# A chain of attention, SwiGLU layer and gated product on one core: w1's second-half left factors made in the late stage, preparation steps held behind the main pipeline

## The chip, the cores and the metric

The kernel runs on one core of a Trainium2 chip. The metric is the device time of one execution in microseconds; before the change the median of 3 runs is 1453.51 us (1453.17 to 1454.55). Beside these runs one execution was recorded by the hardware profiler; the rows below come from it. The core's engines, each with a queue of its own that it works off in order: TensorE (PE, matmuls), VectorE (DVE), ScalarE (ACT), GpSimd (POOL) and SyncE (SP, which here only issues DMA transfers). ACT issues some transfers too.

## The reference

```python
a1 = softmax(p k^T / 8) v            # 32 packed rows per head; 8 batches, 8 heads, 576 rows, head_dim 64
x  = softmax(q a1^T / 8) a1          # then reshaped to 4608 x 512
h  = x @ w_in                        # 512 x 2048
x2 = (h * sigmoid(h)) @ w_out        # 2048 x 512
a, b = x2 @ w1, x2 @ w2              # 512 x 1024 each
out  = ((a * b) @ w3) @ w_out2       # 1024 x 1024, then 1024 x 512
```

All in float32. The kernel folds the last two weights into one, w34 = w3 @ w_out2, before it uses them.

## The kernel before

Every float32 matmul is done as three: each operand is split into a high part, which the engine takes at full pace, and the low part that is left (`split`: the high part a copy on ACT or, with `on_vector`, a cast on DVE; the low part a subtraction on DVE, or on POOL with `eng=G`), and `mm3` (L97) adds high x high, low x high and high x low.

**First product (attention and SwiGLU), to about 877 us.** The main loop runs over 256 items (b, f, m): batch, half of its 576 rows, and one of 16 blocks of 128 columns of w_in. For item i, `emit_h` makes h in a PSUM bank ps_h (6 matmuls of 288 columns), `emit_g` makes sg = tanh(h/2) on ACT, gg = (sg + 1) h on DVE (the gate), its high part gh on ACT and its low part gl on POOL, and `emit_x2` for item i - 3 adds gh and gl times w_out to four PSUM banks ps_x (12 matmuls). ps_h has two banks, so PE can be about two items ahead of the gate. `fetch` loads the left operands of h (mr) and splits them into the slots mq.

Beside the items run three streams of other work, called a step at a time by the loop at the pace of `due`. One is attention for later batches. In the z stream, `decode_late` turns the first MID = 20 blocks of a list `late` of weight blocks from packed 64-bit words to float32 and stores them to DRAM (late_d). From item 209 to item 250 the x stream runs `prepare_second` (L942), the **late stage**. Its `step` takes the next block of the list: it loads it (z from late_d, or raw words from the input, which `Decode` turns with two ACT copies, two DVE operations at L176 and L178, and a POOL add), and then

- a block of w_out2 ("o") is split into o, high part on DVE (tile wo in the rows),
- a block of w3 ("3") is kept for `turn`, which splits it into w3T, and `product`, which multiplies it with o on PE into ps_w: 12 matmuls of 512 columns per w3 block, 16 blocks; every second one is split into w34s and stored,
- a block of w1 or w2 ("12") is kept for `combine`, which with its partner makes the **left factors**: the second product multiplies 2 x 2 blocks with seven multiplications in place of eight (Strassen), for which each pair of blocks needs four sums (DVE, tile sums, L933) and seven parts. Each part is split (tile w12s: high part on ACT, low part on DVE) and stored to DRAM (w12_d) by a transfer that ACT issues. `later` holds these small steps, `some(2)` runs two of them at a time.

w1 and w2 have two column halves. Each half has four combines (w1 and w2, two row pairs each). The late stage makes those of the first half. The blocks of the second half are only decoded.

**Second product, from about 877 us.** 36 items (9 groups of 512 rows, 4 column pairs mp). `emit_ab` makes seven products (12 matmuls of 256 columns each) into ps_ab, sums them on DVE (r), multiplies a and b and splits the result (abh on ACT, abl on DVE); `emit_o` multiplies the previous item's with w34 into ps_o (24 matmuls of 512 columns). Column pairs 0 and 1 use the left factors of the first half, which `load_second` (L1126) loads. Those of pairs 2 and 3 (tile w_23) are made in place by `last_left_factors` (L1139) during the first two items, with the low parts on POOL, from decoded blocks that `load_z12` loads. The memory of w_23 comes free when the last xs of the first product has been stored.

**What sets the order.** A scheduler orders the instructions of each engine's queue by its own model of their times, within the data dependences. `tc.issue_after(ins)` adds that an instruction on the engine of `ins` stands behind `ins`. `behind` holds the latest of some of them: `behind["sg"]` the tanh, `behind["gg"]` the gate. The late stage's steps have no such bound before the change.

## Time and profile before

| what | value |
|---|---|
| median of 3 runs | 1453.51 us |
| profiled execution | 1451.29 us, of which the span from first to last instruction is 1449.5 us |
| PE busy | 1397.1 us (96%) |
| DVE busy | 908.6 us (63%) |
| ACT busy | 672.1 us (46%) |
| POOL busy | 598.6 us (41%) |
| mean granted TensorE clock | 0.991 of full |
| DMA | 193.07 MB, mean 133 GB/s |

Busy times are shares of the span; matmuls are pipelined and their recorded durations overlap, so PE counts as busy while it only works off what it holds, and its real pace is read from start to start. The granted clock of a stretch is a mean of the two levels of TensorE's clock, 2.4 GHz (1.00) and 1.2 GHz (0.50).

### The profile page before, as it was taken

What the parts mean: (1) busy time and instruction counts of PE and PEld (TensorE: products, weight loads), DVE (VectorE), ACT (ScalarE), POOL (GpSimd) and SP (SyncE); (2) the same over time, 40 slices, a digit from 0 to 9 for tenths busy, and PEclk for the clock granted to TensorE, in tenths of its full rate; (3) what the DMA queues carried; (4) which work ended last, traced back from release to release, by engine and by line L of the source; (5) the groups of instructions that cost most, each with busy time, mean ns of one, the idle gap of its engine ahead of it and who ended that gap; (6) DMA issues with size and microseconds to landing.
All of it is one profiled execution on the core that took longest, in us unless ns stands there. A gap on an engine that the chain in (4) does not pass through costs nothing.

```text
span 1449.5 us, 25884 instructions
## 1 busy us (share of the span) xinstructions
PE 1397.1 (96%) x9548; PEld 1310.8 (90%) x9548; DVE 908.6 (63%) x1695; ACT 672.1 (46%) x1466; POOL 598.6 (41%) x626
## 2 busy tenths in 40 slices
PE   7799899999999999999989999999999999999998
PEld 5488799899999999999878998899999999999998
DVE  5897866569775588667897435745364454545453
ACT  6866555565665556654465433422132232323221
POOL 3778755856879657686476333300000000000000
PEclk9999999999999999999999999999999999999999
DMA  8597545845567444562686339011010101101000
GB/s 317 192 311 247 170 140 168 264 139 151 161 205 226 142 134 141 168 181 86 231 267 203 108 133 355 9 59 30 30 59 1 59 12 48 48 12 59 1 30 30
DMA packets 135967, 193.07 MB, mean 133 GB/s; under 512 B 14496, under 2 KB 92576, under 8 KB 135328
## 3 DMA queue, kind: packets, MB, share of 16 engines
q1 hardware_dynamic: 125344, 178.82, 38.4%
q10 hardware_dynamic: 10496, 12.59, 2.5%
q8 instruction: 75, 1.23, 0.3%
q14 instruction: 52, 0.43, 0.1%
HBM read 132.38 MB, written 58.98 MB: 132 GB/s over the span
## 4 chain that ended last, share of the span: by engine, by line
PE 68%; DVE 12%; DMA 7%; ACT 5%; issue 4%; POOL 2%; SPq 2%; ACTq 0%; DVEq 0%; POOLq 0%
PE ps_ab L1225 24%; PE ps_x L100 5%; PE ps_x L98 5%; PE ps_x L99 5%; PE ps_o L98 5%; PE ps_o L99 5%; PE ps_o L100 5%; PE ps_h L98 3%; PE ps_h L100 3%; PE ps_h L99 3%; DVE gg L838 1%; SPq L108 1%; DMA z<-late_d 1%; DVE sbd L244 1%; DVE mq L86 1%
## 5 line engine op out<-in xcount | busy, mean ns | idle before, releaser
L98 PE MATMUL ps_x<-gh,wo 128*128 128x288 f32 x1024 | 303.2, 300 | 6.2 <-DVE xs L875 2.0
L99 PE MATMUL ps_x<-gh,wo 128*128 128x288 f32 x1024 | 301.3, 297 | 0.0
L100 PE MATMUL ps_x<-gl,wo 128*128 128x288 f32 x1024 | 285.9, 298 | 2.3 <-POOL gl L91 2.2
L91 POOL TENSOR_TENSOR gl<-gg,gh 128x288 fp32r<-128x288 f32 x256 | 227.5, 892 | 110.9 <-ACT gh L82 94.9
L1225 PE MATMUL ps_ab<-xct,w 128*128 128x256 f32 x1728 | 222.3, 283 | 1.4 <-DVE r L1246 1.4
L1225 PEld LDWEIGHTS ps_ab<-xct,w 128*128 128x128 f32 x1728 | 214.9, 190 | 2.6 <-DVE r L1246 1.6
L98 PEld LDWEIGHTS ps_x<-gh,wo 128*128 128x128 f32 x1024 | 194.3, 190 | 11.4 <-DVE xs L875 3.6
L82 ACT ACTIVATE gh<-gg 128x288 fp32r<-128x288 f32 x256 | 112.7, 443 | 183.1 <-DVE gg L838 174.5
L99 PEld LDWEIGHTS ps_x<-gh,wo 128*128 128x128 f32 x1024 | 194.4, 190 | 2.2 <-issue 1.2
L100 PEld LDWEIGHTS ps_x<-gl,wo 128*128 128x128 f32 x1024 | 187.7, 190 | 5.5 <-POOL gl L91 4.3
L91 POOL TENSOR_TENSOR mq<-mr,mq 128x256 fp32r<-128x256 f32 x168 | 131.2, 781 | 113.7 <-DVE mq L86 47.1
L1225 PE MATMUL ps_ab<-xcb,w 128*128 128x256 f32 x1296 | 177.2, 283 | 0.0
L98 PE MATMUL ps_h<-a,mq 128*128 128x288 f32 x512 | 156.5, 306 | 21.4 <-DVE gg L838 17.2
L838 DVE SCALAR_TENSOR_TENSOR gg<-sg,ps_h 128x288 f32<-128x288 f32 x256 | 114.5, 447 | 96.1 <-ACT sg L833 48.8
L1225 PEld LDWEIGHTS ps_ab<-xcb,w 128*128 128x128 f32 x1296 | 168.1, 189 | 4.3
L1246 DVE TENSOR_TENSOR r<-p,ps_ab 128x512 f32<-128x512 f32 x72 | 49.2, 683 | 182.9 <-PE ps_ab L1225 182.7
L99 PE MATMUL ps_h<-a,mq 128*128 128x288 f32 x512 | 152.4, 298 | 0.0
L100 PE MATMUL ps_h<-a,mq 128*128 128x288 f32 x512 | 152.0, 297 | 0.1
L833 ACT ACTIVATE sg<-ps_h 128x288 f32<-128x288 f32 x256 | 102.7, 404 | 62.1 <-PE ps_h L100 44.1
L98 PEld LDWEIGHTS ps_h<-a,mq 128*128 128x128 f32 x512 | 96.8, 189 | 30.9 <-DVE gg L838 24.0
L82 ACT ACTIVATE p<-ps_ab 128x512 f32<-128x512 f32 x72 | 43.1, 598 | 145.5 <-PE ps_ab L1225 139.1
L99 PE MATMUL ps_o<-w,abl 128*128 128x512 f32 x280 | 110.0, 393 | 0.0
(173 smaller groups left out, 2649.2 us busy)
## 6 DMA issues: line engine op xcount, KB each, us to landing
mr<-m_d SPq DMA_DIRECT2D x144, 128.0 KB, 2.6
raw<-in_moe_w_dram SPq DMA_DIRECT2D x32, 512.0 KB, 4.4
wz<-wi_d SPq DMA_DIRECT2D x48, 256.0 KB, 3.7
m_d<-ms SPq DMA_DIRECT2D x96, 128.0 KB, 3.0
x_d<-xs SPq DMA_DIRECT2D x20, 576.0 KB, 3.6
raw<-in_moe_w_out_dram SPq DMA_DIRECT2D x22, 512.0 KB, 4.2
out_dram<-ob SPq DMA_DIRECT2D x36, 256.0 KB, 2.0
vr<-in_v_dram SPq DMA_DIRECT2D x14, 640.0 KB, 4.1
```

What stands on the lines that cost most here:

```text
L82: A.activation(out=dst, in_=src, func=ACTF.Copy, scale=mul)
L86: V.tensor_copy(out=hi, in_=src)
L91: (eng or V).tensor_tensor(out=lo, in0=src, in1=hi.bitcast(F32), op=ALU.subtract)
L98: T.matmul(out=dst, lhsT=wh, rhs=xh, start=start, stop=False)
L99: T.matmul(out=dst, lhsT=wl, rhs=xh, start=False, stop=False)
L100: T.matmul(out=dst, lhsT=wh, rhs=xl, start=False, stop=stop)
L108: return eng.dma_start(out=out, in_=in_)
L244: (act_copy if plain else V.tensor_copy)(dst[r, 0, :, r], src[r])
L833: ins = A.activation(out=sg, in_=ps, func=ACTF.Tanh, scale=0.5)
L838: ins = V.scalar_tensor_tensor(out=gg, in0=sg, scalar=1.0, in1=ps, op0=ALU.add, op1=ALU.mult)
L1225: T.matmul(out=bank[:, x], lhsT=w[:, wp], rhs=xt[:, kt, xp], start=first and (x, kt, n) == (0, 0, 0), stop=last and (x, kt, n) == (1, 1, 2 ...
L1246: V.tensor_tensor(out=dst, in0=p, in1=q, op=op)
```

## The change

The list `late` begins with only KEPT = 4 blocks that wait for the second product, those of w2's second half. The four w1 blocks of the second half join the ones that the late stage combines: 6 combines there in place of 4, 2 in the second product in place of 4. w12_d becomes one tensor per half, and `load_second` also loads w1's part for column pairs 2 and 3. The high parts of o move from DVE to ACT. New: `hold(...)` puts a step's instructions behind the latest tanh and gate (and, for `turn` and `product`, behind the latest matmul into ps_h); `due_w3` takes a step only when the w3 block that is needed next is behind it in the list; `some(3)` in place of `some(2)`; and the last left factors run two steps per turn, not four.

```diff
@@ -97,9 +97,16 @@
     def mm3(dst, wh, wl, xh, xl, start, stop):
         T.matmul(out=dst, lhsT=wh, rhs=xh, start=start, stop=False)
         T.matmul(out=dst, lhsT=wl, rhs=xh, start=False, stop=False)
-        T.matmul(out=dst, lhsT=wh, rhs=xl, start=False, stop=stop)
+        return T.matmul(out=dst, lhsT=wh, rhs=xl, start=False, stop=stop)
 
     behind = {}
+
+    def hold(*names):
+
+        stack = ExitStack()
+        for x in names:
+            stack.enter_context(tc.issue_after(behind[x]))
+        return stack
 
     def move(out, in_, eng=DMA):
 
@@ -131,7 +138,7 @@
     ident = const.tile([128, 128], F32, name="ident")
 
     wi_d = dram.tile([4, DM, 512], F32, name="wi_d")
-    w12_d = dram.tile([128, 2, 2, 2, 7, 2, 128], F32, name="w12_d")
+    w12_d = [dram.tile([128, 2, 2, 2, 7, 2, 128], F32, name=f"w12_d{half}") for half in range(2)]
     w34_d = [dram.tile([128, 2, 512], F32, name=f"w34_d{i}") for i in range(KM2)]
     late_d = [dram.tile([128, 512], F32, name=f"late_d{n}") for n in range(MID)]
     x2_d = {(b, f): dram.tile([128, CD, HS], F32, name=f"x2_d{b}_{f}") for b in range(B) for f in range(2)}
@@ -821,11 +828,12 @@
         ps = ps_h.tile([128, HS], F32, tag="h", name="ps_h")
         w = slots[:, holds.index((b, m))]
         for x in range(2):
-            mm3(
+            ins = mm3(
                 ps, w[:, x, 0], w[:, x, 1],
                 a2[b][:, x, 0, f * HS:(f + 1) * HS], a2[b][:, x, 1, f * HS:(f + 1) * HS],
                 x == 0, x == 1,
             )
+        behind["h"] = ins.ins
         return ps
 
     def emit_g(i, ps):
@@ -886,16 +894,19 @@
         late_srcs.append((w1, w2)[x][128 * c:128 * c + 128, 512 * half:512 * half + 512])
 
 
-    for n in range(KM2, 2 * KM2):
+    KEPT = 4
+    for n in range(2 * KM2 - KEPT, 2 * KM2):
         late_w12(n)
     for j in range(KM2):
         late.append(("o", j))
         late_srcs.append(wo2[128 * j:128 * j + 128, :])
+    due_w3 = []
     for n in range(2 * KM2):
         late.append(("3", n))
         late_srcs.append(w3[n])
-        if n % 2 == 0:
-            late_w12(n // 2)
+        due_w3.append(len(late) - KEPT)
+        if n % 4 < 3:
+            late_w12(n // 4 * 3 + n % 4)
 
     def decode_late():
 
@@ -947,7 +958,7 @@
             ps_dec, ps_w = bank("ps_dec"), bank("ps_w34")
 
             def load():
-                n = len(zs) + KM2
+                n = len(zs) + KEPT
                 if n < MID:
                     zs.append(dp.tile([128, 512], F32, tag="z", name="z", bufs=6))
                     move(out=zs[-1], in_=late_d[n])
@@ -962,12 +973,12 @@
             def combine(n):
                 z = [z12.pop(2 * n + y) for y in range(2)]
                 sums = dp.tile([128, 4, 256], F32, tag="sums", name="sums", bufs=2)
-                x, kt = divmod(n, 2)
+                half, x, kt = n // 4, n // 2 % 2, n % 2
 
                 def part(j, src):
                     t = dp.tile([128, 2, 2, 128], F32R, tag="w12s", name="w12s", bufs=4)
                     split(t[:, :, 0], t[:, :, 1], src.rearrange("p (j n) -> p j n", j=2))
-                    store(out=w12_d[:, :, x, kt, j], in_=t, age=0)
+                    store(out=w12_d[half][:, :, x, kt, j], in_=t, age=0)
 
                 later.extend(left_factors(z, sums, part))
 
@@ -980,13 +991,13 @@
             def step():
                 n = used[0]
                 used[0] += 1
-                while len(zs) < min(n + 3, len(late) - KM2):
+                while len(zs) < min(n + 3, len(late) - KEPT):
                     load()
-                (kind, i), z = late[n + KM2], zs[n]
-                if n + KM2 >= MID:
+                (kind, i), z = late[n + KEPT], zs[n]
+                if n + KEPT >= MID:
                     z = Decode(z, dp.tile([128, 512], I32, tag="z", name="z", bufs=6), ps_dec).z
                 if kind == "o":
-                    split(o[i][:, 0], o[i][:, 1], z, on_vector=True)
+                    split(o[i][:, 0], o[i][:, 1], z)
                 elif kind == "3":
                     z3[i] = z
                 else:
@@ -1013,17 +1024,20 @@
                     move(out=w34_d[i], in_=t)
 
             for n in range(KM2 + 3):
-                step()
+                with hold("sg", "gg"):
+                    step()
                 yield
             for n in range(2 * KM2 + 2):
-                if n > 1:
-                    product(n - 2)
-                if n < 2 * KM2:
-                    turn(n)
+                with hold("sg", "gg", "h"):
+                    if n > 1:
+                        product(n - 2)
+                    if n < 2 * KM2:
+                        turn(n)
                 for y in range(2):
-                    if used[0] < min(len(late) - KM2, KM2 + 3 + 3 * (n + y) // 2):
-                        step()
-                    some(2)
+                    with hold("sg", "gg"):
+                        if used[0] < (due_w3[min(n + 1 + y, 2 * KM2 - 1)] if n < 2 * KM2 - 2 else len(late) - KEPT):
+                            step()
+                        some(3)
                     yield
             some(len(later))
             flush()
@@ -1124,8 +1138,9 @@
             w34[m] = pool.tile([128, 2, 512], F32R, name=f"w34_{m}")
 
     def load_second(mp):
-        for x in range(2) if mp < 2 else ():
-            move(out=w12[mp][:, x], in_=w12_d[:, mp, x])
+        half, j = divmod(mp, 2)
+        for x in range(2 - half):
+            move(out=w12[mp][:, x], in_=w12_d[half][:, j, x])
         for m in pair(mp):
             move(out=w34[m], in_=w34_d[m])
 
@@ -1138,8 +1153,8 @@
 
     def last_left_factors():
 
-        for n in range(4):
-            x, kt = divmod(n, 2)
+        for n in range(2):
+            x, kt = 1, n
             sums = early.tile([128, 4, 256], F32, tag="sums", name="sums")
 
             def part(j, src):
@@ -1149,8 +1164,6 @@
             for step in left_factors([z12h.pop((n, y)) for y in range(2)], sums, part):
                 step()
                 yield
-            if n < 2:
-                load_z12(n + 2)
 
     def pair(mp):
         half, j = divmod(mp, 2)
@@ -1234,7 +1247,7 @@
         g, mp = items2[i]
         nxt = iter(())
         if i < 2:
-            nxt = (None for _ in range(7) if drain(islice(last_left, 4)) is None)
+            nxt = (None for _ in range(7) if drain(islice(last_left, 2)) is None)
         if mp == MP - 1 and g + 1 < NG:
             nxt = right_factors(g + 1)
         b1, b2, b3, b4 = (ps_ab.tile([128, 2, 256], F32, tag=f"ab{j}", name=f"ps_ab{j}") for j in range(4))
```

How this moves instructions, at three places. `gg<-sg,ps_h` is the gate on DVE; wo are the tiles o, the numbers behind names are the program's.

DVE where the late stage begins, before the change:

```order
L838 SCALAR_TENSOR_TENSOR gg<-sg,ps_h 128x288
L86 CAST wo_0_9878<-z 128x512
L91 TENSOR_TENSOR wo_0_9878<-z,wo_0_9878 128x512
L838 SCALAR_TENSOR_TENSOR gg<-sg,ps_h 128x288
L86 CAST wo_1_9879<-z 128x512
L86 CAST wo_2_9880<-z 128x512
L91 TENSOR_TENSOR wo_1_9879<-z,wo_1_9879 128x512
L86 CAST wo_3_9881<-z 128x512
L91 TENSOR_TENSOR wo_2_9880<-z,wo_2_9880 128x512
L838 SCALAR_TENSOR_TENSOR gg<-sg,ps_h 128x288
```

and with it:

```order
L846 SCALAR_TENSOR_TENSOR gg<-sg,ps_h 128x288 x5
L86 CAST mq<-mr 128x2x128
L91 TENSOR_TENSOR wo_0_9879<-z,wo_0_9879 128x512
L91 TENSOR_TENSOR wo_1_9880<-z,wo_1_9880 128x512
L846 SCALAR_TENSOR_TENSOR gg<-sg,ps_h 128x288
L86 CAST mq<-mr 128x2x128
L883 TENSOR_SCALAR xs<-ps_x_9396 128x288
L91 TENSOR_TENSOR wo_2_9881<-z,wo_2_9881 128x512
```

The casts are gone from DVE, the first low part stands four gates later, and then about one stands between two gates.

DVE with the change, the densest pass of the late stage, between the gates of items 229 and 230:

```order
L846 SCALAR_TENSOR_TENSOR gg<-sg,ps_h 128x288
L944 TENSOR_TENSOR sums<-z 128x256
L86 CAST mq<-mr 128x2x128
L91 TENSOR_TENSOR w3T<-z,w3T 128x512
L183 TENSOR_SCALAR z<-ps_dec 128x512
L185 SCALAR_TENSOR_TENSOR raw<-ps_dec,raw 128x512
L944 TENSOR_TENSOR sums<-z 128x256
L91 TENSOR_TENSOR w12s<-z,w12s 128x2x128 x2
L944 TENSOR_TENSOR sums<-sums,z 128x256
L183 TENSOR_SCALAR z<-ps_dec 128x512
L185 SCALAR_TENSOR_TENSOR raw<-ps_dec,raw 128x512
L944 TENSOR_TENSOR sums<-z,sums 128x256
```

Two more w12s low parts follow before the next gate, fourteen operations in all. The longest such list before the change has fourteen too, between the gates of items 218 and 219.

ACT where the second product begins, before the change:

```order
L82 ACTIVATE w_23_12001<-z_11767 128x2x128
L82 ACTIVATE w_23_12001<-z_11769 128x2x128 x2
L82 ACTIVATE w_23_12001<-sums 128x2x128 x4
L82 ACTIVATE w_23_12001<-z_11771 128x2x128
L82 ACTIVATE w_23_12001<-z_11773 128x2x128 x2
L82 ACTIVATE abh<-r_12019 128x512
L82 ACTIVATE abh<-r_12018 128x512
L82 ACTIVATE r_12189<-ps_ab_12185 128x2x256
L82 ACTIVATE w_23_12001<-sums 128x2x128 x4
```

and with it:

```order
L82 ACTIVATE w_23_12076<-z_11842 128x2x128
L82 ACTIVATE w_23_12076<-z_11844 128x2x128 x2
L82 ACTIVATE w_23_12076<-sums 128x2x128 x4
L82 ACTIVATE w_23_12076<-z_11846 128x2x128
L82 ACTIVATE abh<-r_12096 128x512
L82 ACTIVATE abh<-r_12095 128x512
L82 ACTIVATE w_23_12076<-z_11848 128x2x128 x2
L82 ACTIVATE r_12234<-ps_ab_12230 128x2x256
L82 ACTIVATE w_23_12076<-sums 128x2x128 x4
```

Eight high parts of left factors stand before abh, not ten, and behind these rows there are none left, where before the change fourteen more followed the first fourteen.

## Rows read from the trace of the kernel before

**Rows 1.** Windows: us; busy (count) of PE, PEld, DVE, ACT, POOL; clock; DMA share; GB/s.
```profile
690.00:782.00 92.00, 82.66 (x507) 75.52 (x507) 85.28 (x141) 52.70 (x119) 57.14 (x57) 0.94 0.77 254
782.00:860.00 78.00, 78.00 (x503) 73.04 (x503) 32.95 (x68) 31.52 (x71) 33.89 (x41) 1.00 0.29 97
690.00:860.00 170.00, 160.66 (x1008) 148.55 (x1008) 118.23 (x208) 84.22 (x189) 91.03 (x97) 0.97 0.55 182
876.00:892.00 16.00, 16.00 (x135) 16.00 (x134) 7.02 (x13) 3.60 (x7) 0.05 (x1) 1.00 1.03 393
892.00:916.00 24.00, 20.64 (x115) 18.31 (x114) 16.86 (x21) 11.64 (x31) 21.30 (x24) 0.86 0.49 180
```

**Rows 2.** Timeline of PE around 848 us: start, duration, instruction.
```profile
845.12 0.39 PE L98 MATMUL ps_w<-wo,w3T 128*128 128x512 f32 x1
...
847.85 0.30 PE L98 MATMUL ps_h<-a,mq 128*128 128x288 f32 x1
...
850.23 0.29 PE L98 MATMUL ps_h<-a,mq 128*128 128x288 f32 x1
```

**Rows 3.** Timeline of DVE, gates of items 205 and 250.
```profile
690.08 0.46 DVE L838 SCALAR_TENSOR_TENSOR gg<-sg,ps_h 128x288 f32<-128x288 f32 x1 [0.78 <-ACT sg L833]
...
859.31 0.45 DVE L838 SCALAR_TENSOR_TENSOR gg<-sg,ps_h 128x288 f32<-128x288 f32 x1 [1.93 <-ACT sg L833]
```

**Rows 4.** Groups of DVE, shapes apart, from 690 to 860 us: busy us, mean ns.
```profile
L838 DVE SCALAR_TENSOR_TENSOR gg<-sg,ps_h 128x288 f32<-128x288 f32 x46 | 20.5, 446 | 18.0 <-ACT sg L833 11.5 <-issue 4.5 <-POOL gl L91 2.0
L86 DVE CAST mq<-mr 128x256 fp32r<-128x256 f32 x32 | 17.6, 551 | 2.8 <-DMA mr<-m_d 2.8
L91 DVE TENSOR_TENSOR w12s<-sums,w12s 128x256 fp32r<-128x256 f32 x16 | 14.1, 907 | 0.0
L91 DVE TENSOR_TENSOR w3T<-z,w3T 128x512 fp32r<-128x512 f32 x16 | 14.1, 885 | 8.0 <-ACT w3T L82 8.0
L176 DVE TENSOR_SCALAR z<-ps_dec 128x512 int32<-128x512 int32 x20 | 13.6, 680 | 0.3 <-ACT ps_dec L82 0.2
L178 DVE SCALAR_TENSOR_TENSOR raw<-ps_dec,raw 128x512 int32<-128x512 int32 x20 | 13.5, 677 | 0.0
L91 DVE TENSOR_TENSOR w12s<-z,w12s 128x256 fp32r<-128x256 f32 x12 | 7.2, 616 | 0.8 <-ACT w12s L82 0.8
L91 DVE TENSOR_TENSOR wo<-z,wo 128x512 fp32r<-128x512 f32 x8 | 6.6, 823 | 0.1
L933 DVE TENSOR_TENSOR sums<-z 128x256 f32<-128x256 f32 x8 | 6.5, 821 | 3.0 <-POOL z L182 3.0
L86 DVE CAST wo<-z 128x512 fp32r<-128x512 f32 x8 | 4.3, 543 | 3.2 <-DMA z<-late_d 3.2
L933 DVE TENSOR_TENSOR sums<-sums,z 128x256 f32<-128x256 f32 x4 | 2.8, 695 | 0.0
L933 DVE TENSOR_TENSOR sums<-z,sums 128x256 f32<-128x256 f32 x4 | 2.2, 540 | 0.0
```

**Rows 5.** Tile w12s: duration in ns, minimum, median and maximum.
```profile
L108 ACTq DMA_DIRECT2D w_d<-w12s x28: 520/521/893, 711.8 to 812.4; - x28
L82 ACT ACTIVATE w12s<-sums x16: 400/418/421, 710.0 to 809.8; 128x256 fp32r<-128x256 f32 x16
L91 DVE TENSOR_TENSOR w12s<-sums,w12s x16: 411/878/1535, 717.4 to 811.7; 128x256 fp32r<-128x256 f32 x16
```

**Rows 6.** Timeline of PE at the change of stages.
```profile
897.72 2.04 PE L98 MATMUL ps_o<-w,abh 128*128 128x512 f32 x4 [2.00 <-ACT abh L82]
...
910.34 3.73 PE L1225 MATMUL ps_ab<-xct,w 128*128 128x256 f32 x19 [1.36 <-DVE r L1246]
```

**Rows 7.** Timeline of ACT at the change of stages.
```profile
893.97 1.03 ACT L82 ACTIVATE w<-z 128x256 fp32r<-128x256 f32 x3 [1.88 <-DMA x_d<-xs]
...
897.05 1.14 ACT L82 ACTIVATE abh<-r 128x512 fp32r<-128x512 f32 x2
```

**Rows 8.** DMA issues: KB each, median us from issue to landing.
```profile
w<-w_d SPq DMA_DIRECT2D x4, 1792.0 KB, 13.9
```

## The prediction, made before the changed kernel had run

> **What bounds the kernel now.** I read the windows by stage first, then TensorE's timeline, then the groups of VectorE (DVE), then the waits at the change of stages. TensorE (PE) is the bound almost everywhere: from 782 to 860 us it is busy all the time at a granted clock of 1.00 [rows 1]. Two places are not like that. From 690 to 782 us DVE is busy 85.28 of 92 us while PE is idle 9.3 us and its granted clock is 0.94, a mean of 1.2 and 2.4 GHz [rows 1]. From 892 to 916 us, where the second product begins, PE is busy 20.64 of 24 us at 0.86 [rows 1].
>
> How much time do they lose? PE's own pace is read where it never waits: 12 matmuls of 512 columns take 847.85 - 845.12 = 2.73 us, 18 of 288 columns 850.23 - 847.85 = 2.38 us [rows 2]. One pass over an item (6 matmuls into ps_h, 12 into ps_x) is 2.38 us. Between the gate of item 205 at 690.08 and that of item 250 at 859.31 us [rows 3] (counted back from item 255, the last) lie 45 passes and all 16 w3 products: 45 x 2.38 + 16 x 2.73 = 150.8 us of PE work in 169.2 us. **Lost in the late stage: 18.4 us**, and before 782, as PE is full behind it.
>
> Why: the stretch's preparation stands on DVE's queue in front of the gates. In the old order the eight casts of w_out2, their low parts, decodes and left factors stand up to fourteen between two gates from item 205 on, long before the products need them. PE then waits for gg. Behind 782 us DVE is busy only 32.95 of 78 us [rows 1]: the work is there, but too early.
>
> At the change of stages PE waits 2.00 us for abh and 1.36 us for DVE's r [rows 6]. ACT had stood until 893.97 us for the store of xs, then ran ten copies into w_23 before abh at 897.05 [rows 7]. The second wait stems from the same left factors: DVE's sums, which wait for POOL's low parts, stand in front of r.
>
> **The change part by part.**
>
> *Holding the steps and due_w3.* Every preparation instruction now stands behind the latest tanh on ACT, gg on DVE and ps_h group on PE, and steps are taken when a w3 block needs them. In the new order DVE has five gates in a row where the casts began, and one low part of wo2 per pass afterwards. From item 205 to 219 DVE's list is 20.1 us long (14 gates, 10 mq, 8 wo2 low parts, 2 xs, 1 w3T, each by its row [rows 4], xs priced as a gate) against 14 x 2.38 = 33.3 us of PE: no loss there.
>
> *Eight wo2 casts go from DVE to ACT.* 8 x 0.543 = 4.3 us leave DVE [rows 4]. ACT, busy 84.22 of 170 us [rows 1], hides 8 copies of at most two 256-wide ones each, 0.84 us [rows 5]; without that cover they would cost 6.7 us.
>
> *Two more combines in the late stage.* DVE gets 14 low parts (8 x 0.907 + 6 x 0.616 = 11.0 us) and 8 sums (4 x 0.821 + 2 x 0.695 + 2 x 0.540 = 5.8 us) [rows 4]; ACT 14 high parts at 0.418 and 14 store issues at 0.521 us, 13.1 us together [rows 5]. Net on DVE +12.5 us: its list from item 205 to 250 grows from 131.3 us (rows 4, and 8 w34s and 6 xs priced as L178 and gg) to 143.8 us. As neighbours overlap, 131.3 of listed time were 118.23 us of busy time [rows 1], a factor of 0.90, so 129 us against 150.8 us of PE. It fits as a whole, but not everywhere. From item 219 to 247 the new order puts on DVE 28 gates, 20 mq, 24 and 18 low parts of w12s, 24 sums, 15 w3T, 20 + 20 decode steps, 7 w34s and 4 xs: 120.6 us listed, 108.5 us net. PE has 28 x 2.38 + 15 x 2.73 = 107.6 us there. So DVE and PE are level for 28 passes; in the densest pass fourteen operations stand between two gates. Waits come on top. In the old stretch DVE was idle 92 - 85.28 = 6.7 us, 7% [rows 1], and its excess over PE plus these waits made the loss. Scaled to 108.5 us these are 7.9 us: 0.9 + 7.9, **I take 8.8 us lost** in place of 18.4, as the old stretch is the nearest row there is. Gain 9.6. Ends: 1 us lost (the excess alone) and 18 (as before).
>
> The price of those DVE ops is where the doubt is. The low part of w12s takes 411 ns at least, 878 in the middle, 1535 at most [rows 5]. The Trainium skill (SBUF — State Buffer, Who interferes with whom) says that a VectorE instruction with two SBUF inputs and a GpSimd instruction that reads SBUF exclude each other, the later one standing fully blocked; it speaks against putting more such work beside a busy GpSimd. By that rule the added ops are to be priced with their stretched durations; the sum by it is the one made here, 1440.4 us, and without it that of the rival "bare" below, 1432.6 us. This trace agrees with it: 411 against 1535 ns for one shape.
>
> *SP and DMA in the late stage.* Four more loads of decoded blocks and 14 more stores of 256 KB, 4.7 MB in 170 us, beside 182 GB/s moved and a DMA share of 0.55 [rows 1]: hidden. POOL's work there is unchanged.
>
> *Late decoding.* The same 20 blocks are decoded early, in another order; nothing is added, 0 us.
>
> *The second product.* 14 copies on ACT, 14 low parts on POOL, 8 sums on DVE and 4 loads go. The new ACT order has eight copies into w_23 before abh, not ten: 0.6 us earlier at some 0.31 us from copy to copy (ten from 893.97 to 897.05 [rows 7]). The wait for the xs store ahead of them stays, so most of the first PE wait stays. The second wait goes: fewer sums stand before r, and POOL ends 14 parts sooner. PE loses there 3.4 us idle plus up to 3.4 us of work at 1.2 GHz (0.86 over 24 us is 6.7 us at half pace) [rows 1, 6]. Half of both, about 3, and 0.5 make **3.5 us gained**. Ends: 6.8, and a loss, from the new loads: two of 1792 KB for w1's part stand on SP behind the xs store. The first is third in line, 2816 KB, 7.3 us at 393 GB/s [rows 1], so at 901.3 us at the earliest. PE wants it after the 24 ps_o matmuls and 12 of 256 columns: 897.7 + 5.5 + 1.4 = 904.6. If it lands as slowly as such loads did, 13.9 us from issue [rows 8], it comes at 908 us: PE waits 3.5 us, and as much again goes at the lower clock behind it. The lower end is -3.5.
>
> Sum: 9.6 + 3.5 = 13.1 us. The profiled execution took 1451.29 us (span 1449.5 and 1.8 around it): 1438.2. The median of the runs is 2.2 us higher, 1453.51, so **1440.4 us**.
>
> **The rivals.**
>
> "Bare": the stretched durations ease, as gates and POOL's parts no longer pile up. With the 42 low parts and 24 sums at 0.41 in place of 50.1 us the list is 97.6, net 87.8 against 107.6: 1 us lost, gain 17.4 + 3.5, **1432.6**. For it: PE and DVE would drift apart only seldom. Against: POOL's parts in these passes stay the same in number.
>
> "Given back": waits between ACT and DVE double. Each of the 42 stores on ACT stands behind its low part on DVE, and tanh and gh stand behind the store; 0.9 + 15.8 = 16.7 us are lost in the late stage, and the 1792 KB load comes late enough to eat the 3.5 us: 18.4 - 16.7 = 1.7, **1451.8**. For it: ACT and DVE both have over 40 more instructions where PE has least slack. Against: in the old stretch ACT was busy 52.70 of 92 us [rows 1].
>
> "Blocked": slower. DVE and POOL take turns so often in items 219 to 247 that the 66 low parts and sums, 0.76 us on average [rows 4], take 1.15: 70.5 + 75.9 = 146.4 listed, 131.8 net, 24.2 over PE; with 7.9 us of waits 32.1 us are lost, 13.7 more than now, less 3.5: **1463.7**. It turns slower by over 0.2% where 18.4 + 3.5 + 2.9 = 24.8 us are lost, 124.5 net, 138.3 listed: at a mean of 1.03 us. For it: single ones reach 1.535 us [rows 5]. Against: a mean a third above the one measured, with no more POOL work than before.
>
> "Not done": the queues keep the hoisted order. Against it stands the order itself; if so, 1453.
>
> **How the numbers follow.** Forecast (1434 to 1447) 0.60, bare 0.20, given back 0.12, blocked 0.06, not done 0.02. Range 1431 to 1450: it takes in bare and most ways between the forecast and given back; left out are blocked, not done and most of given back, some 0.18. A measurement here can tell about 0.2%, 2.9 us. Faster: forecast, bare and a quarter of given back, 0.83; same 0.10; slower 0.07.
>
> **What would show it.** Right: from 690 to 720 us PE busy throughout; DVE near 100% from about 730 to 835 rather than 700 to 780; gates one by one, not in pairs; 42 w12s stores; the span between gates 205 and 250 near 159 us; at the second product one wait for abh of about 1.5 us and none for r. Wrong: the stretch of items 219 to 247 taking over 120 us, a granted clock under 0.95 there, w12s low parts over 1 us on average, or PE waiting for the 1792 KB loads.

## The result, and the profile after

The changed kernel took 1438.99 us (median of 4 runs, 1435.87 to 1440.92), the kernel before beside it 1453.34 us: a ratio of 0.990, 95% interval 0.988 to 0.992. The forecast was 1440.4 us, range 1431 to 1450. The profiled execution took 1435.87 us, with a span of 1434.1 us.

The windows of the kernel after, with the columns of [rows 1] (busy time and count of PE, PEld, DVE, ACT, POOL, then clock, DMA share, GB/s):
```profile
690.00:720.00 30.00, 30.00 (x228) 30.00 (x227) 14.53 (x31) 15.11 (x37) 19.98 (x22) 1.00 0.69 228
720.00:782.00 62.00, 60.08 (x379) 56.17 (x379) 53.97 (x98) 37.05 (x88) 40.04 (x39) 0.97 0.74 235
782.00:860.00 78.00, 75.34 (x477) 70.17 (x476) 58.08 (x104) 43.68 (x101) 39.64 (x40) 0.98 0.68 227
690.00:860.00 170.00, 165.41 (x1080) 156.35 (x1079) 126.58 (x232) 95.83 (x223) 99.66 (x101) 0.98 0.71 230
878.00:902.00 24.00, 22.20 (x156) 20.50 (x156) 15.41 (x21) 10.04 (x23) 11.87 (x14) 1.00 0.88 340
```
From 690 to 720 us PE is full; before the change it was busy 27.87 of these 30 us. DVE's work is spread: 53.97 of 62 us and then 58.08 of 78, in place of 85.28 of 92 and then 32.95 of 78 [rows 1]. The change of stages (last row) keeps the clock at 1.00, where it was 0.86.

The gates of items 205, 219, 247 and 250, DVE's timeline of the kernel after (start, duration, instruction, and in brackets idle time before it and what ended that):
```profile
689.12 0.46 DVE L846 SCALAR_TENSOR_TENSOR gg<-sg,ps_h 128x288 f32<-128x288 f32 x1 [0.78 <-ACT sg L841]
...
722.44 0.45 DVE L846 SCALAR_TENSOR_TENSOR gg<-sg,ps_h 128x288 f32<-128x288 f32 x1 [1.14 <-POOL mq L91]
...
838.93 0.45 DVE L846 SCALAR_TENSOR_TENSOR gg<-sg,ps_h 128x288 f32<-128x288 f32 x1 [3.34 <-ACT sg L841]
...
848.89 0.46 DVE L846 SCALAR_TENSOR_TENSOR gg<-sg,ps_h 128x288 f32<-128x288 f32 x1 [1.93 <-ACT sg L841]
```
From 205 to 250 it is 848.89 - 689.12 = 159.8 us, where it was 169.2 [rows 3]: 9.5 us less, and 9.0 us over PE's own 150.8. All of that is lost behind item 219: from 205 to 219 PE's pace is kept (33.3 us for 14 passes of 2.38), from 219 to 247 it is 116.5 us against 107.6. From gate 250 to the end it is 1434.1 - 848.89 = 585.2 us, before 1449.5 - 859.31 = 590.2: 5.0 us less. The two gains make 14.5 us, as the medians do (14.4); the profiled executions lie 15.4 us apart, of which 1.0 stands before gate 205.

DVE's groups for the left factors of the kernel after, from 690 to 860 us (busy us, mean ns, idle before), which answer to [rows 4]:
```profile
L91 DVE TENSOR_TENSOR w12s<-sums,w12s 128x256 fp32r<-128x256 f32 x24 | 15.8, 678 | 1.3 <-ACT w12s L82 1.3
L91 DVE TENSOR_TENSOR w12s<-z,w12s 128x256 fp32r<-128x256 f32 x18 | 13.2, 749 | 0.0
L944 DVE TENSOR_TENSOR sums<-z 128x256 f32<-128x256 f32 x12 | 7.7, 642 | 0.6 <-POOL z L189 0.6
L944 DVE TENSOR_TENSOR sums<-sums,z 128x256 f32<-128x256 f32 x6 | 4.7, 783 | 0.0
L944 DVE TENSOR_TENSOR sums<-z,sums 128x256 f32<-128x256 f32 x6 | 2.5, 414 | 0.0
```
Counts times means, as in the prediction, these 66 operations are 44.6 us, 0.68 each. And the waits of PE at the change of stages, which answer to [rows 6]:
```profile
886.96 1.20 PE L98 MATMUL ps_o<-w,abh 128*128 128x512 f32 x4 [1.54 <-ACT abh L82]
...
897.40 3.14 PE L1238 MATMUL ps_ab<-xct,w 128*128 128x256 f32 x24 [0.26 <-DVE r L1259]
```

### The profile page after: what moved, and what is told of

Same layout as the page of the kernel before. It is cut to its first block, busy times and chain, and to the rows that moved or that the text cites. A ratio compares the mean times of both kernels' runs of the same rounds, so it can differ in the third digit from the quotient of the medians.

```text
span 1434.1 us, 25927 instructions
## 1 busy us (share of the span) xinstructions
PE 1390.1 (97%) x9548; PEld 1307.3 (91%) x9548; DVE 903.1 (63%) x1701; ACT 672.7 (47%) x1474; POOL 592.0 (41%) x612
## 4 chain that ended last, share of the span: by engine, by line
PE 68%; DVE 12%; DMA 6%; ACT 5%; issue 5%; POOL 2%; SPq 2%; ACTq 0%; DVEq 0%; POOLq 0%
PE ps_ab L1238 24%; PE ps_x L100 6%; PE ps_x L98 5%; PE ps_x L99 5%; PE ps_o L98 5%; PE ps_o L99 5%; PE ps_o L100 5%; PE ps_h L98 3%; PE ps_h L100 3%; PE ps_h L99 3%; SPq L115 2%; DMA m_d<-ms 1%; DVE gg L846 1%; DVE sbd L251 1%; DMA z<-late_d 1%
## 5 line engine op out<-in xcount | busy, mean ns | idle before, releaser
L100 PE MATMUL ps_x<-gl,wo 128*128 128x288 f32 x1024 | 289.5, 297 | 1.5 <-POOL gl L91 1.4
L1238 PE MATMUL ps_ab<-xct,w 128*128 128x256 f32 x1728 | 219.4, 282 | 0.3 <-DVE r L1259 0.3
L82 ACT ACTIVATE gh<-gg 128x288 fp32r<-128x288 f32 x256 | 112.7, 443 | 167.2 <-DVE gg L846 157.3
L91 POOL TENSOR_TENSOR mq<-mr,mq 128x256 fp32r<-128x256 f32 x168 | 136.7, 814 | 115.4 <-DVE mq L86 57.5
L100 PE MATMUL ps_o<-w,abh 128*128 128x512 f32 x280 | 109.5, 391 | 0.0
```

The source lines that it names most:

```text
L82: A.activation(out=dst, in_=src, func=ACTF.Copy, scale=mul)
L91: (eng or V).tensor_tensor(out=lo, in0=src, in1=hi.bitcast(F32), op=ALU.subtract)
L100: return T.matmul(out=dst, lhsT=wh, rhs=xl, start=False, stop=stop)
L1238: T.matmul(out=bank[:, x], lhsT=w[:, wp], rhs=xt[:, kt, xp], start=first and (x, kt, n) == (0, 0, 0), stop=last and (x, kt, n) == (1, 1, 2 ...
```

## The experiments

All are told by the same two stretches of their profiles, gate 205 to gate 250 (PE's own work in it is 150.8 us in each) and gate 250 to the end, since where gate 205 lies differs by up to 4 us between executions (689.1 to 692.8 in those of kernels that differ only behind it). Ratios are to the kernel before, run beside them.

Two columns say where the first stretch loses: "PE idle", the waits of PE that the profile lists in it, and "clock", the stretch times what its mean granted clock is short of 1.00. What is left beyond 150.8 us and these two, 0.8 to 4.1 us, no row tells. They are those of the one profiled execution; the mean clock of whole executions differs within a kernel (e7: 0.990 to 0.994). How well do the stretches repeat? f1 and f3 differ only behind gate 250 and take 154.5 and 154.9 us to it; the eight kernels with the second product of the change take 584.8 to 586.7 us behind it.

| kernel | 205 to 250 | PE idle | clock | 250 to end | median | ratio, 95% interval |
|---|---|---|---|---|---|---|
| before | 169.2 | 9.2 | 5.1 | 590.2 | 1453.34 | |
| after | 159.8 | 4.6 | 3.4 | 585.2 | 1438.99 | 0.9901 (0.9879 to 0.9924) |
| e1_no_hold | 168.3 | 11.0 | 3.4 | 585.2 | 1448.21 | 0.9968 (0.9956 to 0.9981) |
| e2_hold_only | 153.8 | 2.0 | 0.0 | 590.2 | 1439.10 | 0.9907 (0.9893 to 0.9920) |
| e3_kept8 | 153.8 | 1.9 | 0.0 | 591.0 | 1438.81 | 0.9904 (0.9890 to 0.9917) |
| e4_cast_dve | 159.7 | 4.6 | 3.4 | 586.5 | 1437.24 | 0.9891 (0.9878 to 0.9905) |
| v3_spread | 157.2 | 3.6 | 0.0 | 584.8 | 1434.17 | 0.9871 (0.9857 to 0.9886) |
| e8_some2 | 158.5 | 4.0 | 1.7 | 585.2 | 1437.20 | 0.9891 (0.9873 to 0.9909) |
| e5_half_pool | 157.3 | 4.5 | 0.0 | 586.7 | 1438.00 | 0.9902 (0.9885 to 0.9918) |
| e7_store_sp | 154.7 | 2.6 | 0.0 | 585.4 | 1434.95 | 0.9877 (0.9862 to 0.9892) |
| f1_spread_sp | 154.5 | 2.4 | 0.0 | 585.2 | 1432.99 | 0.9868 (0.9850 to 0.9886) |
| f2_kept8_sp | 151.8 | 0.2 | 0.0 | 590.8 | 1437.53 | 0.9899 (0.9881 to 0.9917) |
| f3_later | 154.9 | 2.8 | 0.0 | 586.8 | 1433.76 | 0.9869 (0.9853 to 0.9885) |

### Which part of the change pays

**e1_no_hold**, the change without its hold:
```diff
     def hold(*names):
-        stack = ExitStack()
...
-        return stack
+        return ExitStack()
```


> The changed kernel with hold() doing nothing; all else stays (late factors, due steps, casts on ACT). Theory (the order on DVE makes the late gain): DVE's list from item 205 to 230 is 90.7 us again, 81.6 net, against 73.2 us of PE work, and with waits 17 to 22 us are lost from gate 205 to 250 (span 168 to 173 us); the second product keeps its 5 us: 1447 to 1453 us. Rival (less work on DVE, the casts and the pace, makes the gain, not the order): 1439 us as the changed kernel, span 159.8 us.

Measured: 168.3 and 585.2 us, 1448.21 us. DVE's gates of items 205 and 219 in its timeline:
```profile
692.58 0.45 DVE L843 SCALAR_TENSOR_TENSOR gg<-sg,ps_h 128x288 f32<-128x288 f32 x1 [0.78 <-ACT sg L838]
...
743.03 0.44 DVE L843 SCALAR_TENSOR_TENSOR gg<-sg,ps_h 128x288 f32<-128x288 f32 x1
```
They lie 50.5 us apart, not 33.3, and the second did not wait for an input: DVE itself was late. PE takes 45.0 us from its item 205 to its item 219, since it can run two items ahead of the gate. Without the hold 17.5 us are lost in the late stage, within the theory's 17 to 22, and 0.9 us of its gain are left; the 5 us of the second product stay.

**e2_hold_only**, the kernel before with nothing but the hold lines of the diff:
```diff
...
-                step()
+                with hold("sg", "gg"):
+                    step()
...
+                with hold("sg", "gg", "h"):
...
+                    with hold("sg", "gg"):
...
+                        some(2)
```


> The kernel before with hold() alone: the old steps, casts on DVE, four blocks of left factors of w1 and w2 still in the second product. Theory (order): list of items 219 to 247 is 102.2 us, 92 net against 107.6 us of PE, so only waits are lost: 3 to 8 us from gate 205 to 250 (span 154 to 159 us); the second product takes 590 us from gate 250 as before: 1439 to 1443 us. Rival (less work makes the gain): span 166 us or more, 1450 us or more.

**e3_kept8**, the change with w1's second half left in the second product:
```diff
-    KEPT = 4
+    KEPT = 8
...
-        if n % 4 < 3:
-            late_w12(n // 4 * 3 + n % 4)
+        if n % 2 == 0:
+            late_w12(n // 2)
...
-                        some(3)
+                        some(2)
...
-        for x in range(2 - half):
+        for x in range(2 if half == 0 else 0):
...
-        for n in range(2):
-            x, kt = 1, n
+        for n in range(4):
+            x, kt = divmod(n, 2)
...
+            if n < 2:
+                load_z12(n + 2)
...
-            nxt = (None for _ in range(7) if drain(islice(last_left, 2)) is None)
+            nxt = (None for _ in range(7) if drain(islice(last_left, 4)) is None)
```


> The changed kernel with w1's second half left in the second product (KEPT = 8, load_second and last_left_factors as before): hold, due steps and casts on ACT stay. Theory (the moved factors cost a little late and pay at the second product): span of gates 205 to 250 154 to 158 us, 2 to 5 us less than the changed kernel; from gate 250 to the end 590 us, 5 more; 1438 to 1442 us. Rival (the moved factors cost nothing late): span 159.8 us, 1444 us. Second rival (the second product gained by something else than the moved factors, such as the clock): 585 us from gate 250, 1434 to 1437 us.

Both took 153.8 us from gate 205 to 250, just under the 154 that their theories gave as the least: holding alone gains 15.4 us in the late stage, and the loss falls from 18.4 to 3.0. Both keep some 590 us behind it. As e2 and e3 agree, the due steps and the casts on ACT gain nothing that shows. And **the factors of w1, for which the change is named, pay nothing that shows here**: they cost 159.8 - 153.8 = 6.0 us in the late stage (PE's waits grow by 2.7, the clock's part by 3.4) and give 5.0 (e2) to 5.8 us (e3) at the second product. The times agree: 0.9901 with them, 0.9907 and 0.9904 without.

The windows of e3_kept8 and its PE waits between 870 and 920 us (total, times, longest) show what the second product pays for them:
```profile
896.00:902.00 6.00, 5.05 (x27) 4.92 (x28) 5.23 (x7) 2.58 (x6) 6.00 (x8) 0.72 0.00 0
```
```profile
PE ps_o L98 <- ACT abh L82: 1.3, 1, 1.3
PE ps_ab L1240 <- DVE r L1261: 1.3, 1, 1.3
PE ps_ab L1240 <- ACT w L82: 0.9, 2, 0.5
```
Four short waits, and at the last of them the granted clock is 0.72 for 6 us; in the kernel after two waits are left and the clock stays at 1.00.

**e4_cast_dve**, the eight wo2 casts back on DVE:
```diff
-                    split(o[i][:, 0], o[i][:, 1], z)
+                    split(o[i][:, 0], o[i][:, 1], z, on_vector=True)
```


> The changed kernel with the eight wo2 casts on DVE as before. Theory (they stand in items 205 to 219, where DVE has 20 us of list against 33 us of PE work): no change, 1439 us within 1.5, PE full from 690 to 720 us still. Rival (DVE's work counts wherever it stands): 4.3 us slower, 1443 us.

Measured: 33.3 us from item 205 to 219, 159.7 to 250, and a time within the interval of the change (1.8 us under the 1439 named, away from the rival). 4.3 us of work on DVE cost nothing where DVE has slack; that they moved was worth nothing either.

### What the 9 us that are still lost are made of

PE's waits between 690 and 860 us (total, times, longest) in the kernel after:
```profile
PE ps_w L98 <- DVE w34s L91: 2.7, 1, 2.7
PE ps_h L98 <- DVE gg L846: 1.9, 1, 1.9
```
PE waits only twice, and behind each wait its clock falls (0.76 from 770 to 777 us, 0.78 from 820 to 826). By the windows of the result the clock costs 62 x 0.03 + 78 x 0.02 = 3.4 us, so that 4.6 of waits and 3.4 of clock make 8.0 of the 9.0 us.

The wait for gg, at 770.61 us, ends the densest pass, between the gates of items 229 and 230. On DVE:
```profile
760.51 0.44 DVE L846 SCALAR_TENSOR_TENSOR gg<-sg,ps_h 128x288 f32<-128x288 f32 x1
760.87 1.45 DVE L944 TENSOR_TENSOR sums<-z 128x256 f32<-128x256 f32 x1
...
764.69 1.87 DVE L91 TENSOR_TENSOR w12s<-z,w12s 128x256 fp32r<-128x256 f32 x2
...
768.35 1.84 DVE L91 TENSOR_TENSOR w12s<-sums,w12s 128x256 fp32r<-128x256 f32 x2
770.12 0.44 DVE L846 SCALAR_TENSOR_TENSOR gg<-sg,ps_h 128x288 f32<-128x288 f32 x1
```
It takes 9.61 us, without idle time on DVE, where PE has 2.38 of matmuls for the pass and at most a product of 2.73 beside it. Yet over 722 to 839 us DVE is busy only 101.53 of 117 us. The other wait hangs on ACT, where the high part of w34s stands behind two w12s stores:
```profile
815.76 1.46 ACTq L115 DMA_DIRECT2D w_d<-w12s  x2
817.32 0.60 ACT L82 ACTIVATE w34s<-ps_w 128x512 fp32r<-128x512 f32 x1 [2.07 <-DVE z L183]
818.70 0.50 PE L98 MATMUL ps_w<-wo,w3T 128*128 128x512 f32 x1 [2.66 <-DVE w34s L91]
```
So I asked of the density (v3, e8), of DVE's work (e5) and of ACT's queue (e7).

**e8_some2:**
```diff
-                        some(3)
+                        some(2)
```


> The changed kernel with two left-factor operations per step in place of three; same work in the same stretch, the densest pass falls from 10.3 to 7.3 us of DVE list, others grow (220 to 234 and 245 to 248). Theory (single dense passes stop PE): gates 205 to 250 in 156 to 158 us, 1435 to 1437 us. Rival (the sum over the stretch decides, 116 us of list either way): 159.8 us, 1439 us.

158.5 us, 1.3 less than the change, just outside either theory's number; 1437.20 us can't be told from it. The clock gave back 1.7 us, and PE's waits are 4.0 us in place of 4.6. Thinning single passes helps little.

**v3_spread:**
```diff
         late.append(("o", j))
         late_srcs.append(wo2[128 * j:128 * j + 128, :])
+        if j % 2:
+            late_w12(j // 2)
...
-        if n % 4 < 3:
-            late_w12(n // 4 * 3 + n % 4)
+        if n % 2 == 0:
+            late_w12(4 + n // 2)
...
-                    step()
+                    for _ in range(2 if n in (1, 3, 5, 7) else 1):
+                        step()
+                    some(2)
...
-                        some(3)
+                        some(2)
```


> The changed kernel with the late blocks in another order: a block of w1 or w2 after every second wo2 block, two blocks in four of the first eleven steps, and two left-factor operations per step from there on. No work is added or removed. Theory (the moved factors cost late time because they are packed where DVE and PE are level): items 205 to 219 carry 33.3 us of DVE list in place of 20.1 (PE 33.3), items 219 to 247 105.6 in place of 118.8 (PE 107.6), the densest pass 8.0 in place of 10.3; gates 205 to 250 take 154 to 157 us, from gate 250 on 585: 1433 to 1436 us. Rival (their cost is the sum of the work, wherever it stands): 159.8 us, 1439 us.

157.2 us, just over the theory's upper end, 1434.17 us. By the gates it takes 38.2 us from item 205 to 219, 4.9 more than the change, and 109.0 from there to 247. But gate 219 stands 5.1 us behind PE's start on its item here, and 1.6 in the change: since that stretch has become as full (33.3 of list against 33.3), DVE is late at its end, while PE runs on. PE itself takes 34.7 us from item 205 to 219, 1.4 more than in the change, and 112.6 from 219 to 247, 3.9 less. Its waits are 3.6 us in place of 4.6, and the clock's 3.4 us came back. Work moved out of a crowd must go where there is slack, and part of it went into a new crowd.

**e5_half_pool:**
```diff
-                    split(t[:, :, 0], t[:, :, 1], src.rearrange("p (j n) -> p j n", j=2))
+                    split(t[:, :, 0], t[:, :, 1], src.rearrange("p (j n) -> p j n", j=2), eng=G if j % 2 else None)
```


> The changed kernel with 18 of the 42 low parts of w12s on POOL. Theory (DVE's list bounds the stretch): 13 us of list leave DVE, items 219 to 247 fall to 106 us; gates 205 to 250 take 154 to 157 us, 1433 to 1436 us. Rival (POOL, busy 72 of 117 us, gets late with mq and the decode that DVE waits for, and its low parts take over 1 us each): 160 us or more, 1439 to 1445 us.

157.3 us, just over the theory's upper end, but not by its mechanism: items 219 to 247 take 114.0 us, not 106, and PE's waits are 4.5 us, as in the change. The clock gave back 3.4 us in this execution; the time, 1438.00 us, is that of the change. So that less work on DVE alone helps is not shown. Tile w12s in it (ns, minimum, median, maximum):
```profile
L91 DVE TENSOR_TENSOR w12s<-z,w12s x12: 412/856/1031, 724.4 to 824.7; 128x256 fp32r<-128x256 f32 x12
L91 POOL TENSOR_TENSOR w12s<-sums,w12s x12: 731/916/1192, 728.6 to 830.9; 128x256 fp32r<-128x256 f32 x12
L91 DVE TENSOR_TENSOR w12s<-sums,w12s x12: 410/807/1022, 730.9 to 831.1; 128x256 fp32r<-128x256 f32 x12
```
and in the kernel after:
```profile
L91 DVE TENSOR_TENSOR w12s<-sums,w12s x24: 410/460/1507, 728.3 to 831.4; 128x256 fp32r<-128x256 f32 x24
L91 DVE TENSOR_TENSOR w12s<-z,w12s x18: 407/424/1533, 723.4 to 827.1; 128x256 fp32r<-128x256 f32 x18
```
With POOL busier (85.82 of 113 us in place of 69.89) the median low part that stays on DVE takes 0.81 to 0.86 us, not 0.42 to 0.46; the mean is 0.77, not 0.71. The casts of mq lengthen too, from 0.453 to 0.576 us. So DVE is busy 95.73 us in place of 100.87, 5.1 less, where 18 low parts at the mean are 12.8. What DVE is spared in number it pays in part in length. In the kernel after, the 14 low parts that overlap no instruction of POOL take 0.41 to 0.43 us, the other 28 0.41 to 1.53, median 0.96. The rule cited in the prediction (the Trainium skill, SBUF — State Buffer, Who interferes with whom) agrees with these rows.

**e7_store_sp:**
```diff
-    def store(out, in_, age=1):
-
-        stores.append([age, out, in_])
+    def store(out, in_, age=1, eng=A):
+
+        stores.append([age, out, in_, eng])
...
-                move(x[1], x[2], A)
+                move(x[1], x[2], x[3])
...
-                    store(out=w12_d[half][:, :, x, kt, j], in_=t, age=0)
+                    store(out=w12_d[half][:, :, x, kt, j], in_=t, age=0, eng=DMA)
```


> The changed kernel with the 42 stores of w12s issued from SP instead of ACT. Theory A (tanh stands on ACT behind stores that wait for DVE's low parts, 9.2 us in items 219 to 247, and that makes part of the loss): gates 205 to 250 in 155 to 158 us, 1434 to 1437 us. Theory B (DVE's list alone makes the loss): 159.8 us, 1439 us. Rival (a store that waits on SP stands before the loads of the next blocks, and these come late): over 161 us, 1441 us or more.

154.7 us, 5.1 less than the change, 1434.95 us; all but one of its runs (1433.38 to 1436.79) lie below all of the change. ACT's largest wait in sum between 722 and 838 us (total, times, longest) in the kernel after:
```profile
ACT sg L841 <- DVE w12s L91: 9.2, 4, 3.6
```
and in e7_store_sp:
```profile
ACT sg L841 <- PE ps_h L100: 11.4, 12, 3.0
```
The row of 9.2 us is gone. A tanh needs nothing from w12s; it stood behind a store, and the store waited on ACT for DVE's low part. The longest of these four waits, on ACT:
```profile
806.49 3.00 ACTq L115 DMA_DIRECT2D w_d<-w12s  x3
809.54 0.41 ACT L841 ACTIVATE sg<-ps_h 128x288 f32<-128x288 f32 x1 [3.56 <-DVE w12s L91]
```
Not all of it is waiting: the three stores took 1.7 of these 3.56 us to issue, and in all four waits the issuing makes 4.5 of the 9.2 us. e7 takes both off ACT. Now tanh waits for its own ps_h, so PE is the one that is late, as it should be. DVE's wait for tanh falls with it, between 720 and 836 us from
```profile
DVE gg L846 <- ACT sg L841: 5.6, 8, 1.4
```
in the kernel after to
```profile
DVE gg L846 <- ACT sg L841: 1.7, 2, 1.1
```
in e7_store_sp. PE's waits from 690 to 860 us and the window of the stage in e7_store_sp:
```profile
PE ps_w L98 <- DVE w34s L91: 1.5, 2, 1.3
PE ps_h L98 <- DVE gg L846: 1.0, 1, 1.0
```
```profile
690.00:850.00 160.00, 157.43 (x1043) 148.75 (x1042) 122.94 (x226) 93.43 (x216) 99.58 (x100) 1.00 0.68 224
```
The wait of 2.7 us that stood behind stores is 0.2 here; those of the densest pass stay (1.0 and 1.3 in place of 1.9). Of the 5.1 us, 2.0 are waits of PE and 3.4 the clock, which is 1.00 throughout, with 0.3 lost elsewhere. SP bears the waiting stores without a loss: theory A comes nearest (0.3 us under its range), and theory B and the rival fall. How much of it was waiting for DVE, as theory A says, and how much the time to issue is not shown. The Trainium skill (DMA: Bandwidth & Descriptors, Anatomy of one DMA — SWDGE (gpsimd) path) says that DMA engines don't wait on semaphores, but the sequencer that issues does, before it dispatches. The rows from 806.49 us, of stores that ACT issues, agree.

### Both remedies, and whether the factors can be made to pay

**f1_spread_sp** is v3_spread with the diff of e7_store_sp, **f2_kept8_sp** is e3_kept8 with it.

> Both remedies together: the late blocks spread as in v3_spread and the w12s stores on SP as in e7_store_sp. Theory (dense passes and the stores in front of tanh are two losses): gates 205 to 250 in 152 to 154 us, from gate 250 on 585: 1430 to 1433 us. Rival (both take away the same waits): 154.7 us, 1434 to 1436 us.

> e3_kept8 (w1's second half left in the second product) with the w12s stores on SP. Theory (moving w1's factors pays 5 us at the second product and costs in the late stage only what its order loses): gates 205 to 250 in 151.5 to 153.5 us, 590 to 591 us from gate 250: 1436 to 1438 us, 4 us over f1_spread_sp. Rival (the moved factors pay nothing): level with f1_spread_sp within 1.5 us.

f1 takes 154.5 us, the rival's span: PE takes 33.3 us from item 205 to 219 and 111.3 from there to 247, in e7 33.3 and 111.4, so with the stores off ACT the spread adds nothing in this stage. Its 1432.99 us is the lowest median of the study and lies in the theory's range. All its runs (1431.62 to 1435.30) lie below all of the change (1435.87 to 1440.92); against v3_spread and e7_store_sp alone the intervals overlap, so that the two add is not shown.

f2 takes 151.8 us, 1.0 over PE's own work, and 590.8 behind it: 1437.53 us, 4.5 over f1 in the same comparison. With the stores on SP, the factors cost 154.5 - 151.8 = 2.7 us there and give 590.8 - 585.2 = 5.6 at the second product. Against e7, which like f2 is without the spread, it is 2.9 and 5.4. So they pay, but only once the stores stand off ACT's queue.

**f3_later** starts w2's factors only in the second item of the second product:
```diff
-        if i < 2:
-            nxt = (None for _ in range(7) if drain(islice(last_left, 2)) is None)
+        if i == 1:
+            nxt = (None for _ in range(7) if drain(islice(last_left, 4)) is None)
```


> f1_spread_sp with w2's left factors made only in the second item of the second product, four operations at each place in place of two. Theory (abh waits on ACT behind the copies into w_23, and these behind the store of xs): PE's wait of 1.4 us for abh shrinks below 0.5, and from gate 250 on it takes 582 to 584 us; 1 to 3 us faster than f1_spread_sp. Rival (the same work, packed twice as densely, stands in front of r on DVE or comes late for the third item): 586 to 590 us from gate 250, slower than f1_spread_sp.

The rival's number came, 586.8 us, but not by its mechanism: PE waits neither for r nor for the third item's factors of w2. The time, 1433.76 us, can't be told from f1's. The wait for abh is gone, as planned, and PE comes sooner to w1's left factors, which have not landed. PE's timeline and the window around it:
```profile
890.88 2.33 PE L1242 MATMUL ps_ab<-xcb,w 128*128 128x256 f32 x12 [2.30 <-DMA w<-w_d]
```
```profile
890.00:894.00 4.00, 3.12 (x17) 3.15 (x18) 3.93 (x6) 1.43 (x3) 3.03 (x4) 0.70 1.07 453
```
This is the late transfer that the prediction kept as its lower end: in the kernel after the wait for abh covered it. There it landed at 893.73 us, 9.1 us from its issue, and the matmuls that read it start at 894.10, so that 0.4 us were in hand. f1 and e4_cast_dve wait for such loads already:
```profile
891.30 1.66 PE L1242 MATMUL ps_ab<-xcb,w 128*128 128x256 f32 x12 [0.51 <-DMA w<-w_d]
```
```profile
895.92 1.67 PE L1238 MATMUL ps_ab<-xcb,w 128*128 128x256 f32 x12 [0.76 <-DMA w<-w_d]
```
The clock of f3 falls as well, to 0.70 in these 4 us.

## Why the prediction was right, and where not

- **Late stage, gain 9.6:** 9.5 measured. From item 205 to 219 no loss was forecast, and there was none. 42 stores of w12s, gates one by one, a clock of 0.97 from 722 to 839 us: as foretold.
- **Its inner working failed, and that its number came out is luck.** The step "0.9 + 7.9" took DVE and PE as level, with DVE near 100%. The 66 low parts and sums took 44.6 us, not 50.1, and DVE was busy 101.5 us from item 219 to 247, not 108.5, so it had 6 us less to do than PE. It was idle 15.0 us, not 7.9: the waits, scaled from the old stretch, were too small by 7.1 us, and DVE's work was too large by 7.0. The whole loss of 8.9 us there is waits and what hangs on them, not an excess: at PE 4.6 us of waits, 3.4 of the clock, for which the sum had no term, and 0.9 that no row tells. More than half of it (5.1, e7) went when the stores left ACT's queue, where they stood in front of tanh and of w34s. That is the mechanism of the rival "given back", at half its price.
- **The parts were not priced apart.** The prediction gave one gain for hold and moved factors together. Apart they are 15.4 and -6.0 in the late stage (e2, e3). The 12.5 us net on DVE stood in the sum as work that fits as a whole; that it would cost 6.0 us was not said.
- **wo2 casts:** without effect, as they lie in slack (e4).
- **The second product, 3.5:** 5.0 measured, within its ends of 6.8 and -3.5. The abh wait was forecast near 1.5 us (1.54) and r's gone (0.26). Too small was the clock's share: half of 3.4 us was taken, and the clock stayed at 1.00. PE's idle time in 24 us fell from 24 - 20.64 = 3.4 [rows 1] to 24 - 22.20 = 1.8, and 24 x (1 - 0.86) = 3.4 us came back from the clock: 1.6 + 3.4 = 5.0, as measured. As the same second product takes up to 1.5 us more in other executions (e4, e5), so close a match is in part chance. Against e3, where PE was busy 33.37 us from 875 to 912 us and 35.20 in the kernel after, the same sum gives 1.8 + 6 x (1 - 0.72) = 3.5 of 5.8 us; the rest is open.
- **1792 KB loads:** no wait in the profiled execution of the kernel after, but with 0.4 us in hand; in e4, f1 and f3 PE does wait for such loads (0.5 to 2.3 us). The lower end was nearer than the sum made it look.
- **"Bare", "blocked", "not done":** a mean of 0.68 us lies between bare (0.41) and the 0.76 forecast, far from 1.03. POOL's instructions between gates 205 and 250 stayed 97, as the prediction said, but took 96.83 us, not 91.03. The order was moved as the kernel says (e1).

## What to carry to other kernels

Price each part of a change by itself: here the ordering (15.4 us) carried one that, by itself, came out even. Before work is moved to another stage, compare the lists of the two engines gate by gate, not over the stage, and look where the moved DMAs stand: a store on a compute engine's queue makes that engine wait for the store's producer, and whatever stands behind it too. Count with a wait of TensorE what its clock takes behind it (3.4 of the 9.0 us here). A wait that is taken away shows the next one (f3), so know how late that is.

## What was not expected of the hardware

One wait of 1.54 us at the change of stages left the granted clock at 1.00 (878 to 902 us, kernel after); one of 2.30 us came with 0.70 over 4 us (f3), four of 0.4 to 1.3 us with 0.72 over 6 us (e3). In the late stage one of 1.93 us came with 0.76 over 7 us (kernel after), while one of 1.95 us in v3 left it at 1.00: by these rows the length of one wait alone does not tell. And another issuing engine for 42 stores of 0.52 us was worth 5.1 us in the late stage. By the Trainium skill (Trainium Kernel Development and Optimization, Key Constraints) issuing from several engines concurrently saves only the sequencer's issue time. Here that is some 22 us on ACT, and the waits of the stores for DVE left ACT with it; no run tells the two apart.
